# Reading the moving columns of every MLP product alternately from the two halves of their 512

## The chip, the cores and the metric

One NeuronCore of a Trainium2 chip runs the kernel. Its engines are TensorE (PE in the profile; PEld is its loading of weights), VectorE (DVE), ScalarE (ACT), GpSimd (POOL) and SyncE (SP, which issues all the DMAs here). The metric is the device time of one execution in microseconds (us). A matmul multiplies a stationary operand of 128 x 128 with a moving operand of 128 partitions x N columns and writes N columns into one bank of PSUM; the other engines read PSUM and work in SBUF.

## What is computed

Pooled attention, then two MLPs, all in float32. Cut to its core:

```python
k_p = k.reshape(B, H, S // 8, 8, D).mean(axis=3)      # B, H, S, D = 8, 8, 576, 64
v_p = v.reshape(B, H, S // 8, 8, D).mean(axis=3)
attn = softmax(q @ k_p.T / sqrt(D)) @ v_p
x = attn.transpose(0, 2, 1, 3).reshape(4608, 512)
h = x @ w_in;  x = (h * sigmoid(h)) @ w_out           # w_in 512 x 2048, w_out 2048 x 512
h = x @ w_in2; out = (h * clip(h + 3, 0, 6) / 6) @ w_out2
```

## The kernel before

The 4608 tokens are cut into 9 groups of 512 (GT), the 2048 inner columns into 16 slices of 128 (NF). A step is one slice f of one group g of one layer; there are 2 x 9 x 16 = 288 of them, in the order layer, group, slice. The order of all instructions on each engine is written out by hand in the loop at lines 627 to 703.

A float32 value is kept as two float32r parts, a high and a low one (xh and xl, gh and gl, and the two halves of whl for weights), and each product of two such values takes three matmuls: high by high, low by high, high by low.

- h_mm (L410, matmul at L416): the first product of a step. Four blocks of 128 of the 512 inputs by three matmuls, 12 in all, each with a moving operand of 128 x 512: 512 tokens of xh or xl. They add up in one bank, hps; there are two such banks.
- act_a (L425): ScalarE reads the bank into t (L428 in layer 1, L433 in layer 2) and VectorE combines t with the bank (L429, L434). act_b (L439) splits t: ScalarE writes gh (L442), VectorE gl (L443).
- y_mm (L446, matmul at L460): the second product, of the step before; the loop calls it through pend. Four banks y0 to y3 by three matmuls, 12 in all. In layer 1 the weights are stationary and gh or gl (512 tokens) moves, so that the result stands transposed for layer 2; in layer 2 gh or gl is stationary and 512 weight columns move. The four banks add up over the 16 slices of a group.
- y_out (L464) at the end of a group: ScalarE empties y0 and y2 (L469), VectorE y1 and y3 (L471), and SyncE stores them.

So TensorE runs 12 matmuls of h_mm(f), then 12 of y_mm(f-1), then 12 of h_mm(f+1), and the activations of f have all of y_mm(f-1) and h_mm(f+1) to finish in.

Beside the steps of group g in layer 1 the attention of group g+1 is worked, one tile of 128 tokens at a time: scores (L266, matmul L276), the softmax on VectorE and ScalarE (L289 to L329), the transposition (in group 0 by TensorE, L340; later by VectorE, L357, and a way through DRAM), weighted (matmul L380), and split_x (L388), which makes xh (L396) and xl (L397) of the next group. In group 0 the weights of layer 1 come in and are turned from their raw words into high and low parts (L92 to L116); later in layer 1 the same is done for layer 2's weights in pieces (L138 to L158).

At the start, while the first loads arrive, warm_wide (L248) runs matmuls on a tile of zeros, probe, to bring up TensorE's clock: 20 of float32r with 512 columns read straight (L252), 10 of bfloat16 read straight (L254), 10 of float32r whose 512 columns are read alternately from the two halves of the tile (L257), and 10 of bfloat16 with every second word (L259). keep_warm (L261, matmul L264) goes on from there, then come the scores of the first four tiles. pool_k (L193) has filled kbd for them by then, at L206.

Of the kernel before, what the change touches and what calls it, by code (L numbers as in the profile page):

```python
# [12 lines left out]
AF = mybir.ActivationFunctionType  # L13
ALU = mybir.AluOpType
# [10 lines left out]
def kernel(  # L25
# [14 lines left out]
    nc = tc.nc  # L40
    B, NPAIR, P, S = k.shape
# [3 lines left out]
    NF = w_in1.shape[0]  # L45
# [15 lines left out]
    ps_y = ctx.enter_context(tc.tile_pool(name="ps_y", bufs=1, space=PSUM))  # L61
# [4 lines left out]
    three = const.tile([P, 1], F32, name="three")  # L66
# [3 lines left out]
    x1 = [dram.tile([DM, GT], F32, name=f"x1_{g}") for g in range(NG)]  # L70
    blocks = [dram.tile([P, NB, H, Q], F32, name=f"bl{i}") for i in range(2)]
    w2 = [[dram.tile([P, 2, DM], F32, name=f"w2_{f}_{p}") for p in range(2)] for f in range(NF)]


    w_raw = {}
# [164 lines left out]
    def bank(tags, i):  # L240
        pool, tag = tags[i]
        return pool.tile([P, 512], F32, tag=tag, name="aps")
# [2 lines left out]

    probe = p2.tile([P, 512], F32R, tag="o", name="probe", bufs=4)

    def warm_wide(ps, ns):  # L248

        half = probe.bitcast(mybir.dt.bfloat16)  # L250
        for n in range(ns):
            nc.tensor.matmul(ps, probe[:, :P], probe, start=True, stop=True)  # L252
        for n in range(10):
            nc.tensor.matmul(ps, half[:, :P], half[:, :512], start=True, stop=True)  # L254
        two = probe.rearrange("p (a f) -> p f a", a=2)
        for n in range(10):
            nc.tensor.matmul(ps, probe[:, :P], two, start=True, stop=True)  # L257
        for n in range(10):
            nc.tensor.matmul(ps, half[:, :256].rearrange("p (f w) -> p f w", w=2)[:, :, 1], half.rearrange("p (f w) -> p f w", w=2)[:, :, 1], start=True, stop=True)  # L259

    def keep_warm(ps, n):  # L261

# [147 lines left out]
    def h_mm(layer, g, f):  # L410
        ih, il = w_sl[layer, f, 0]
        xh, xl = xs[layer * NG + g]
        ps = ps_h.tile([P, GT], F32, tag="h", name="hps")
        for n, (w, x) in enumerate(((ih, xh), (il, xh), (ih, xl))):
            for c in range(NKC):
                nc.tensor.matmul(  # L416
                    ps,
                    w[:, c, :],
                    x[:, c, :],
                    start=(c == 0 and n == 0),  # L420
                    stop=(c == NKC - 1 and n == 2),
                )
        return ps

    def act_a(layer, ps):  # L425
        t = p2.tile([P, GT], F32, tag="t", name="t")
        if layer == 0:
            nc.scalar.activation(t, ps, AF.Tanh, scale=0.5)  # L428
            nc.vector.scalar_tensor_tensor(  # L429
                out=t, in0=t, scalar=1.0, in1=ps, op0=ALU.add, op1=ALU.mult  # L430
            )
        else:
            nc.scalar.activation(t, ps, AF.Relu, bias=three)  # L433
            nc.vector.scalar_tensor_tensor(  # L434
                out=t, in0=t, scalar=6.0, in1=ps, op0=ALU.min, op1=ALU.mult
            )
        return t

# [7 lines left out]
    def y_mm(layer, g, f):  # L446
        gh, gl = g_t.pop((layer, g, f))
        oh, ol = w_sl[layer, f, 1]
        if f == 0:
            y_ps[layer, g] = [  # L450
                ps_y.tile([P, 512], F32, tag=f"y{i}", name=f"y{i}") for i in range(4)
            ]
        for i, ps in enumerate(y_ps[layer, g]):
            sl = slice(i * P, (i + 1) * P)
            if layer == 0:
                prods = ((oh[:, sl], gh), (ol[:, sl], gh), (oh[:, sl], gl))
            else:
                prods = ((gh[:, sl], oh), (gh[:, sl], ol), (gl[:, sl], oh))
            for n, (a, b) in enumerate(prods):
                nc.tensor.matmul(  # L460
                    ps, a, b, start=(f == 0 and n == 0), stop=(f == NF - 1 and n == 2)
                )

    def y_out(layer, g):  # L464
        scale = 0.5 if layer == 0 else 1.0 / 6.0
        for i, ps in enumerate(y_ps.pop((layer, g))):
            o = p2.tile([P, 512], F32, tag="o", name="o", bufs=4)
            if i % 2 == 0:
                nc.scalar.activation(o, ps, AF.Copy, scale=scale)  # L469
            else:  # L470
                nc.vector.tensor_scalar(  # L471
                    out=o, in0=ps, scalar1=scale, scalar2=None, op0=ALU.mult
                )
            if layer == 0:
                dst = x1[g][i * P:(i + 1) * P, :]
            else:
                dst = out[g * GT + i * P:g * GT + (i + 1) * P, :]
            nc.sync.dma_start(out=dst, in_=o)
# [44 lines left out]
    with tc.manual_schedule():  # L523
# [22 lines left out]
        for i in range(2):  # L546
            nc.gpsimd.memset(kbd[i], 0.0)
        nc.gpsimd.memset(probe.bitcast(F32), 0.0)
        warm_wide(bank(((ps_y, "y0"),), 0), 20)
        make_identity(nc, ident)  # L550
        nc.gpsimd.memset(three, 3.0)
        for i in range(2):
# [74 lines left out]
        for layer in range(2):  # L627
            for g in range(NG):
                todo = stages(g) if layer == 0 else [[] for _ in range(NF)]
                for f in range(NF):  # L630
                    n = (layer * NG + g) * NF + f
# [6 lines left out]
                    while later:  # L638
                        later.pop(0)()
                    ps = h_mm(layer, g, f)  # L640
                    if 1 in now:
                        t1 = now[1]
# [3 lines left out]
                    if 3 in now:  # L646
                        pv = weighted(now[3])
                    tt = act_a(layer, ps)
                    quota = share[n] if n < NF else 2
                    due = len(done)  # L650
# [27 lines left out]
                    if pend is not None:  # L678
                        y_mm(*pend)
                        if pend[2] == NF - 1:  # L680
                            y_out(*pend[:2])
# [8 lines left out]
                    if n >= 5 and layer == 0 and f % 2 == 1:  # L690
# [4 lines left out]
                        if kv_jobs and TPG * (g + 1) + f // 4 + 3 >= first_tile[kv_jobs[0][0]]:  # L695
                            b, j = kv_jobs.pop(0)
# [4 lines left out]
                    if 0 <= s < NF:  # L701
                        load_split(s, 0)
                        load_split(s, 1)
        y_mm(*pend)
        y_out(*pend[:2])


# [46 lines left out]
```

## Time and profile before

| | |
|---|---|
| median of 3 runs | 1772.79 us (1772.59 to 1773.47) |
| the profiled execution | 1772.91 us, its span 1771.1 us |
| granted TensorE clock, mean over the span | 0.994 of full |
| PE busy | 1729.6 us (98%), 8032 matmuls in the records |
| PEld busy | 1388.5 us (78%) |
| DVE busy | 813.2 us (46%) |
| ACT busy | 549.1 us (31%) |
| POOL busy | 254.8 us (14%) |
| MLP matmuls, L416 and L460 | 6912, of 128 x 512 each |

The span is the time from the first to the last instruction of the core; the execution's own time holds some 1.8 us more. Matmuls overlap, so that the mean duration of one is longer than the time from one to the next; the latter is a stretch of the span divided by the matmuls in it. A matmul of plain float32, as those of the attention and of keep_warm, stands in the records as two.

### The profile page before, as it was taken

How to read it: one execution, taken by the hardware profiler on the slowest of the kernel's cores; microseconds unless marked ns; L12 is line 12 of the kernel's file. 1: busy time of each engine (PE TensorE's matmuls, PEld its weight loads, DVE VectorE, ACT ScalarE, POOL GpSimd, SP SyncE). 2: the span in 40 equal slices, each digit the busy share in tenths (PEclk: the TensorE clock that was granted, in tenths of full speed). 3: DMA queues.
4: the chain of work that ended last, by engine and by line, in shares of the span. 5: the costliest groups of instructions: out<-in, count | busy, mean ns of one | idle time of the engine just before them, and what ended most of it. 6: DMA issues, size and time to landing. Idle time of an engine off the chain costs nothing.

```text
span 1771.1 us, 20673 instructions
## 1 busy us (share of the span) xinstructions
PE 1729.6 (98%) x8032; PEld 1388.5 (78%) x8032; DVE 813.2 (46%) x1356; ACT 549.1 (31%) x1007; POOL 254.8 (14%) x258
## 2 busy tenths in 40 slices
PE   8787999999999999999999999999999999999999
PEld 6566887878788888888888888888888888888887
DVE  5999667566665766544322222222222222222222
ACT  4454333333333333222222222222222222222222
POOL 4665222022220222100000000000000000000000
PEclk9899999999999999999999999999999999999999
DMA  8340435343353534211265010101010100000000
GB/s 278 114 163 20 138 123 165 107 144 129 117 168 104 157 124 146 76 67 38 81 200 198 13 36 13 36 13 36 13 36 13 34 14 30 19 22 27 8 17 24
DMA packets 77186, 144.35 MB, mean 82 GB/s; under 512 B 7840, under 2 KB 32288, under 8 KB 77088
## 3 DMA queue, kind: packets, MB, share of 16 engines
q1 hardware_dynamic: 77088, 143.03, 24.7%
q8 instruction: 63, 1.03, 0.3%
q14 instruction: 35, 0.29, 0.1%
HBM read 96.34 MB, written 46.66 MB: 81 GB/s over the span
## 4 chain that ended last, share of the span: by engine, by line
PE 90%; DVE 6%; issue 2%; ACT 1%; POOL 0%; DVEq 0%; ACTq 0%; POOLq 0%
PE y L460 43%; PE hps L416 43%; PE aps L276 2%; PE aps L380 2%; DVE wmag L95 1%; DVE gl L443 1%; DVE wmag L98 1%; DVE t L429 1%; DVE kbd L206 0%; ACT whl L115 0%; PE aps L252 0%; ACT wmag L92 0%; DVE mx L292 0%; DVE den L324 0%; DVE pr L293 0%
## 5 line engine op out<-in xcount | busy, mean ns | idle before, releaser
L416 PE MATMUL hps<-xh,whl 128*128 128x512 f32 x2304 | 585.3, 396 | 3.5 <-POOL whl L116 1.6
L416 PEld LDWEIGHTS hps<-xh,whl 128*128 128x128 f32 x2304 | 434.1, 189 | 107.3 <-POOL whl L116 2.0
L460 PE MATMUL y<-gh,whl 128*128 128x512 f32 x1152 | 372.2, 404 | 1.4 <-POOL whl L116 1.1
L460 PE MATMUL y<-whl,gh 128*128 128x512 f32 x1152 | 361.6, 395 | 0.0
L434 DVE SCALAR_TENSOR_TENSOR t<-t,hps 128x512 f32<-128x512 f32 x144 | 99.1, 688 | 495.4 <-ACT t L433 495.4
L416 PE MATMUL hps<-xl,whl 128*128 128x512 f32 x1152 | 316.1, 396 | 0.8 <-DVE xl L397 0.8
L443 DVE TENSOR_TENSOR gl<-t,gh 128x512 fp32r<-128x512 f32 x288 | 226.7, 787 | 191.2 <-ACT gh L442 190.5
L442 ACT ACTIVATE gh<-t 128x512 fp32r<-128x512 f32 x288 | 182.0, 632 | 269.6 <-DVE t L429 161.0
L416 PEld LDWEIGHTS hps<-xl,whl 128*128 128x128 f32 x1152 | 217.1, 189 | 53.6 <-DVE xl L397 2.1
L460 PEld LDWEIGHTS y<-whl,gh 128*128 128x128 f32 x1152 | 216.3, 188 | 52.3
L460 PEld LDWEIGHTS y<-gh,whl 128*128 128x128 f32 x1152 | 214.2, 190 | 54.4 <-ACT hraw L157 3.7
L433 ACT ACTIVATE t<-hps,three 128x512 f32<-128x512 f32 x144 | 99.1, 688 | 481.4 <-PE hps L416 481.4
L460 PE MATMUL y<-gl,whl 128*128 128x512 f32 x576 | 230.5, 400 | 13.2 <-DVE gl L443 13.2
L460 PE MATMUL y<-whl,gl 128*128 128x512 f32 x576 | 227.4, 395 | 0.0
L429 DVE SCALAR_TENSOR_TENSOR t<-t,hps 128x512 f32<-128x512 f32 x144 | 97.9, 680 | 220.2 <-ACT t L428 219.6
L428 ACT ACTIVATE t<-hps 128x512 f32<-128x512 f32 x144 | 85.9, 596 | 352.9 <-PE hps L416 352.9
L492 POOL TENSOR_TENSOR xl<-xr,xh 128x512 fp32r<-128x512 f32 x36 | 46.5, 1291 | 897.3 <-ACT xh L491 897.3
L460 PEld LDWEIGHTS y<-gl,whl 128*128 128x128 f32 x576 | 109.9, 191 | 41.3 <-DVE gl L443 15.7
L460 PEld LDWEIGHTS y<-whl,gl 128*128 128x128 f32 x576 | 108.2, 188 | 26.0
L158 POOL TENSOR_TENSOR hraw<-hmag,hraw 128x256 fp32r<-128x256 f32 x64 | 47.3, 738 | 424.1 <-ACT hraw L157 328.3
L116 POOL TENSOR_TENSOR whl<-wmag,whl 128x512 fp32r<-128x512 f32 x32 | 50.7, 1601 | 51.9 <-ACT whl L115 51.8
L300 ACT ACTIVATE pr<-pr 128x288 f32<-128x288 f32 x64 | 28.5, 445 | 84.4 <-DVE pr L293 84.4
(78 smaller groups left out, 911.8 us busy)
## 6 DMA issues: line engine op xcount, KB each, us to landing
w<-hraw SPq DMA_DIRECT2D x64, 256.0 KB
whl<-w SPq DMA_DIRECT2D x32, 512.0 KB
bl<-bT SPq DMA_DIRECT2D x28, 384.0 KB
x<-o SPq DMA_DIRECT2D x36, 256.0 KB
xr<-x SPq DMA_DIRECT2D x36, 256.0 KB
out_dram<-o SPq DMA_DIRECT2D x36, 256.0 KB
wraw<-in_moe_w_in_dram SPq DMA_DIRECT2D x16, 512.0 KB
wraw<-in_moe_w_out_dram SPq DMA_DIRECT2D x16, 512.0 KB
```

What stands on the lines that cost most here:

```text
L116: nc.gpsimd.tensor_tensor(out=t[:, 1, :], in0=mag, in1=t[:, 0, :].bitcast(F32), op=ALU.subtract)
L158: nc.gpsimd.tensor_tensor(out=t[:, 1], in0=mag, in1=t[:, 0].bitcast(F32), op=ALU.subtract)
L276: nc.tensor.matmul(ps[o:o + n, jj * PW:(jj + 1) * PW], qT[:, j, o:o + n], kbd[b % 2][:, j, :], start=True, stop=True,)
L416: nc.tensor.matmul(ps, w[:, c, :], x[:, c, :], start=(c == 0 and n == 0), stop=(c == NKC - 1 and n == 2),)
L428: nc.scalar.activation(t, ps, AF.Tanh, scale=0.5)
L429: nc.vector.scalar_tensor_tensor(out=t, in0=t, scalar=1.0, in1=ps, op0=ALU.add, op1=ALU.mult)
L433: nc.scalar.activation(t, ps, AF.Relu, bias=three)
L434: nc.vector.scalar_tensor_tensor(out=t, in0=t, scalar=6.0, in1=ps, op0=ALU.min, op1=ALU.mult)
L442: nc.scalar.activation(gh, t, AF.Copy)
L443: nc.vector.tensor_tensor(out=gl, in0=t, in1=gh.bitcast(F32), op=ALU.subtract)
L460: nc.tensor.matmul(ps, a, b, start=(f == 0 and n == 0), stop=(f == NF - 1 and n == 2))
L492: nc.gpsimd.tensor_tensor(out=xl[:, c, :], in0=r, in1=xh[:, c, :].bitcast(F32), op=ALU.subtract)
```

## The change

Three helpers give other orders to the 512 columns of a tile. shuffled reads column 0, 256, 1, 257 and so on: alternately from the two halves. A matmul whose moving operand is read so writes its 512 results into PSUM in that order, side by side. dealt reads a bank back in the order of the tokens: first every second word from the first on, then every second from the second on. in_two is the plain order, written as two halves so that its shape fits that of dealt.

All MLP matmuls, L416 and L460, now read their moving operand through shuffled. The stationary operands are as before. Every read of a bank of hps or y by ScalarE or VectorE goes through dealt, and what they write in SBUF stands in the old order, so that all else is unchanged. The attention's matmuls are not touched.

The warm-up is another one: 14 float32r matmuls with 512 columns read from the two halves, 10 with 256 columns read from the two halves of 256, and 10 with 512 columns read in turn from the four quarters; no bfloat16 ones. It has 34 matmuls where it had 50. No other instruction of any engine changes its place.

```diff
@@ -70,6 +70,17 @@
     x1 = [dram.tile([DM, GT], F32, name=f"x1_{g}") for g in range(NG)]
     blocks = [dram.tile([P, NB, H, Q], F32, name=f"bl{i}") for i in range(2)]
     w2 = [[dram.tile([P, 2, DM], F32, name=f"w2_{f}_{p}") for p in range(2)] for f in range(NF)]
+    def shuffled(ap):
+        return ap.rearrange("p (a n) -> p n a", a=2)
+    def dealt(ps):
+        return ps.rearrange("p (n a) -> p a n", a=2)
+    def in_two(ap):
+        return ap.rearrange("p (a n) -> p a n", a=2)
 
 
     w_raw = {}
@@ -245,18 +256,17 @@
 
     probe = p2.tile([P, 512], F32R, tag="o", name="probe", bufs=4)
 
-    def warm_wide(ps, ns):
-
-        half = probe.bitcast(mybir.dt.bfloat16)
-        for n in range(ns):
-            nc.tensor.matmul(ps, probe[:, :P], probe, start=True, stop=True)
+    def warm_wide(ps):
+        w = probe[:, :P]
+        for n in range(14):
+            nc.tensor.matmul(ps, w, shuffled(probe), start=True, stop=True)
         for n in range(10):
-            nc.tensor.matmul(ps, half[:, :P], half[:, :512], start=True, stop=True)
-        two = probe.rearrange("p (a f) -> p f a", a=2)
+            nc.tensor.matmul(ps[:, :256], w, shuffled(probe[:, :256]), start=True, stop=True)
         for n in range(10):
-            nc.tensor.matmul(ps, probe[:, :P], two, start=True, stop=True)
-        for n in range(10):
-            nc.tensor.matmul(ps, half[:, :256].rearrange("p (f w) -> p f w", w=2)[:, :, 1], half.rearrange("p (f w) -> p f w", w=2)[:, :, 1], start=True, stop=True)
+            nc.tensor.matmul(
+                ps, w, probe.rearrange("p (a f) -> p f a", a=4), start=True, stop=True
+            )
 
     def keep_warm(ps, n):
 
@@ -416,7 +426,7 @@
                 nc.tensor.matmul(
                     ps,
                     w[:, c, :],
-                    x[:, c, :],
+                    shuffled(x[:, c, :]),
                     start=(c == 0 and n == 0),
                     stop=(c == NKC - 1 and n == 2),
                 )
@@ -424,15 +434,16 @@
 
     def act_a(layer, ps):
         t = p2.tile([P, GT], F32, tag="t", name="t")
+        t2, h = in_two(t), dealt(ps)
         if layer == 0:
-            nc.scalar.activation(t, ps, AF.Tanh, scale=0.5)
+            nc.scalar.activation(t2, h, AF.Tanh, scale=0.5)
             nc.vector.scalar_tensor_tensor(
-                out=t, in0=t, scalar=1.0, in1=ps, op0=ALU.add, op1=ALU.mult
+                out=t2, in0=t2, scalar=1.0, in1=h, op0=ALU.add, op1=ALU.mult
             )
         else:
-            nc.scalar.activation(t, ps, AF.Relu, bias=three)
+            nc.scalar.activation(t2, h, AF.Relu, bias=three)
             nc.vector.scalar_tensor_tensor(
-                out=t, in0=t, scalar=6.0, in1=ps, op0=ALU.min, op1=ALU.mult
+                out=t2, in0=t2, scalar=6.0, in1=h, op0=ALU.min, op1=ALU.mult
             )
         return t
 
@@ -458,7 +469,7 @@
                 prods = ((gh[:, sl], oh), (gh[:, sl], ol), (gl[:, sl], oh))
             for n, (a, b) in enumerate(prods):
                 nc.tensor.matmul(
-                    ps, a, b, start=(f == 0 and n == 0), stop=(f == NF - 1 and n == 2)
+                    ps, a, shuffled(b), start=(f == 0 and n == 0), stop=(f == NF - 1 and n == 2)
                 )
 
     def y_out(layer, g):
@@ -466,10 +477,10 @@
         for i, ps in enumerate(y_ps.pop((layer, g))):
             o = p2.tile([P, 512], F32, tag="o", name="o", bufs=4)
             if i % 2 == 0:
-                nc.scalar.activation(o, ps, AF.Copy, scale=scale)
+                nc.scalar.activation(in_two(o), dealt(ps), AF.Copy, scale=scale)
             else:
                 nc.vector.tensor_scalar(
-                    out=o, in0=ps, scalar1=scale, scalar2=None, op0=ALU.mult
+                    out=in_two(o), in0=dealt(ps), scalar1=scale, scalar2=None, op0=ALU.mult
                 )
             if layer == 0:
                 dst = x1[g][i * P:(i + 1) * P, :]
@@ -546,7 +557,7 @@
         for i in range(2):
             nc.gpsimd.memset(kbd[i], 0.0)
         nc.gpsimd.memset(probe.bitcast(F32), 0.0)
-        warm_wide(bank(((ps_y, "y0"),), 0), 20)
+        warm_wide(bank(((ps_y, "y0"),), 0))
         make_identity(nc, ident)
         nc.gpsimd.memset(three, 3.0)
         for i in range(2):
```

## Rows read from the trace of the kernel before

**Rows 1.** The page: the chain of work that ended last, by line.
```profile
PE y L460 43%; PE hps L416 43%; PE aps L276 2%; PE aps L380 2%; DVE wmag L95 1%; DVE gl L443 1%; DVE wmag L98 1%; DVE t L429 1%; DVE kbd L206 0%; ACT whl L115 0%; PE aps L252 0%; ACT wmag L92 0%; DVE mx L292 0%; DVE den L324 0%; DVE pr L293 0%
```

**Rows 2.** Stretches: bounds, length, busy time (xcount) of each engine, clock, DMA.
```profile
37.00:167.85 130.85, 99.87 (x461) 75.40 (x462) 125.62 (x150) 64.22 (x117) 77.46 (x57) 0.92 0.33 119
167.85:900.00 732.15, 731.37 (x3626) 589.21 (x3626) 441.68 (x834) 237.89 (x475) 117.19 (x138) 1.00 0.37 117
900.00:1771.00 871.00, 867.50 (x3724) 698.90 (x3722) 226.12 (x330) 231.78 (x365) 45.17 (x35) 1.00 0.11 38
11.30:13.46 2.16, 2.16 (x12) 1.66 (x11) 0.00 (x0) 0.00 (x0) 2.00 (x4) 1.00 1.02 263
80.00:160.00 80.00, 63.86 (x336) 49.30 (x334) 76.88 (x96) 40.83 (x75) 44.76 (x33) 1.00 0.29 107
163.50:167.00 3.50, 2.88 (x9) 1.77 (x8) 2.85 (x7) 1.68 (x4) 0.00 (x0) 0.51 0.00 0
```

**Rows 3.** The chain, two blocks: start, us, what.
```profile
412.05 2.80 PE y L460 x12
...
1761.92 5.60 PE y L460 x24
```

**Rows 4.** The chain, the warm-up; second line, the last ten of L252 alone.
```profile
2.34 6.79 PE aps L252 x20
6.82 2.31 PE aps L252 x10
9.13 2.17 PE aps L254 x10
11.30 2.16 PE aps L257 x10
13.46 2.27 PE aps L259 x10
15.73 2.68 PE aps L264 x24
```

**Rows 5.** The same stretch for L416 and for L460 alone: PE, PEld, clock, DMA.
```profile
167.85:1771.00 1603.15, 810.49 (x3288) 617.84 (x3287) 1.00 0.23 74
167.85:1771.00 1603.15, 818.51 (x3300) 616.13 (x3300) 1.00 0.23 74
```

**Rows 6.** Single lines: xcount, ns min/median/max, first and last start.
```profile
L429 DVE SCALAR_TENSOR_TENSOR t<-t,hps x144: 646/689/690, 46.2 to 957.3; 128x512 f32<-128x512 f32 x144
L92 ACT ACTIVATE wmag<-wraw x32: 647/665/698, 32.5 to 168.2; 128x512 f32<-128x512 f32 x32
L115 ACT ACTIVATE whl<-wmag x32: 612/617/632, 35.2 to 174.9; 128x512 fp32r<-128x512 f32 x32
L98 DVE SCALAR_TENSOR_TENSOR wmag<-wraw,wmag x32: 691/694/1715, 33.7 to 171.0; 128x512 uint32<-128x512 uint32 x32
L146 DVE SCALAR_TENSOR_TENSOR hmag<-hraw,hmag x64: 424/425/566, 196.1 to 712.3; 128x256 uint32<-128x256 uint32 x64
```

**Rows 7.** The timeline in layer 2: start, us, engine, what [idle before it].
```profile
1506.84 0.69 DVE L443 TENSOR_TENSOR gl<-t,gh 128x512 fp32r<-128x512 f32 x1 [0.70 <-ACT gh L442]
...
1510.53 0.40 PE L460 MATMUL y<-whl,gl 128*128 128x512 f32 x1
```

**Rows 8.** The timeline of the start.
```profile
9.08 1.51 DVE L206 TENSOR_REDUCE kbd<-stage 64x72 f32<-64x576 f32 x2 [1.42 <-DMA stage<-in_k_dram]
10.57 1.26 POOL L216 TENSOR_TENSOR stage<-stage 72x512 f32<-72x512 f32 x1 [4.06 <-DMA stage<-in_v_dram]
```

**Rows 9.** The timeline in layer 1.
```profile
162.39 0.50 PE L460 MATMUL y<-gl,whl 128*128 128x512 f32 x1 [3.85 <-DVE gl L443]
...
280.63 1.19 PE L416 MATMUL hps<-xl,whl 128*128 128x512 f32 x4 [0.23 <-DVE xl L397]
...
415.66 0.69 DVE L443 TENSOR_TENSOR gl<-t,gh 128x512 fp32r<-128x512 f32 x1 [0.70 <-ACT gh L442]
...
417.96 0.40 PE L460 MATMUL y<-gl,whl 128*128 128x512 f32 x1
```

## The prediction, made before the changed kernel ran

> **What bounds the kernel now.** I read the chain that ended last first. 86% of the span run through the two MLP lines on TensorE, L416 and L460, and 4% more through its attention lines [rows 1]. The reader is to see there that no other engine, and no transfer, holds the end.
>
> A table by stretch then says where that is not so [rows 2]. From 37 to 168 us VectorE is busy 125.6 of 130.9 us and TensorE 99.9. VectorE is converting weights and doing attention beside the first steps, and TensorE waits for it. From 167.85 us on TensorE is busy all the time (731.4 of 732.2 us, then 867.5 of 871, the rest being the last evacuation and store) at a granted clock of 1.00. There the time is the number of matmuls times their pace.
>
> The pace is the number to look at. A row's "mean ns of one" (395 to 404 ns) is no pace, since matmuls overlap. From 900 us to 1767.52, where the last block ends, there are 3724 matmuls [rows 2, 3], which makes 233.0 ns from one to the next; a block of 12 in layer 1 takes 2.80 us, which is 233 ns too [rows 3].
>
> **The change, part by part.**
>
> *The moving reads.* The warm-up before the first real work happens to hold the operation that is now put everywhere [rows 4]. Its first loop has the same matmul as the MLP (float32r, 128 x 512, read straight): once the clock is up ten of them take 2.31 us, 231 ns each, on zeros. The third loop reads the same tile alternately from its two halves: ten take 2.16 us, 216 ns each. Ten straight bfloat16 ones take 2.17 us. So a straight float32r read costs some 15 to 17 ns per matmul that the alternating one does not. That the zeros of the probe pace like the real work when read straight (231 against 233) is my reason to carry the 216 over.
>
> The price: after 167.85 us there are 3288 matmuls of L416 and 3300 of L460 [rows 5], 6588. At 233 - 216 = 17.0 ns each that is 112.0 us. The other 324 (of 288 steps of 24) lie before it and gain nothing, because VectorE sets the time there. Bounds on the new pace: below, the row's own 216, since bfloat16 comes to the same 216 or 217; above, 227, the slowest full-clock group of the warm-up (strided bfloat16, 2.27 us for ten), if the reads meet traffic that the probe lacked; at 227 the gain is 40 us. I take 216, the one row of this very form.
>
> [...] The probe's row shows the scattered read faster than the straight one, 2.16 against 2.31 us for ten [rows 4]. [...]
>
> *The dealt reads of PSUM.* Per step ScalarE and VectorE read the first product's bank once each (VectorE's L429 takes 0.689 us [rows 6]), and per group of 16 steps they empty two of the four y banks each. All now read every second word. The trace has no strided read of PSUM. The nearest rows are strided reads of SBUF: L92 on ScalarE, every second word, 0.665 against 0.617 us for L115, which reads straight; L98 on VectorE, 0.694, against 0.689 for L429 [rows 6]. So the low bound is nothing (a gain is excluded: the same number of elements is read), the next +0.05 us, and the far one a doubling of the part that grows with the elements. That part I get from one shape against half its size: L98's 0.694 us for 512 and L146's 0.425 for 256 [rows 6], 0.27 us per 256, so +0.54 us for 512. I take nothing to 0.05, by the nearest rows. What covers it: in layer 2 gl, the last of the four passes that follow the product, is done at 1506.84 + 0.69 = 1507.53 us, while the matmul that needs it starts at 1510.53 [rows 7]: 3.0 us to spare, 2.6 after 24 matmuls at 17 ns less. Without that cover each step would pay. In the stretch to 167.85 us VectorE has no cover, and 13.5 steps (324 matmuls by 24 a step) would pay 13.5 x 0.54 = 7.3 us at the far bound.
>
> *The warm-up.* Before, it runs from 2.34 to 15.73 us [rows 4], and the chain goes straight through it. Now: 14 matmuls of 512 columns (the first ten 4.48 us, as before, 6.82 - 2.34, then four at 216), ten of 256 and ten of 512 read from four quarters. A 256-column one lies between the 128-column row (2.68 us for 24, 112 ns) and 216; I take 130. The quarters I take at 216, with twice that as the far bound. Sum 4.48 + 0.86 + 1.3 + 2.16 = 8.8 us against 13.39, so 4.6 us less (1.6 us with both far bounds). What is late next? The scores need kbd, whose last reduction ends at 9.08 + 1.51 = 10.6 us [rows 8], and q; the warming at L264 (2.68 us) still lies between, so they start at about 13.8 us. The loads of q and v are queued alternately and v's first lands at 10.57 us [rows 8]; five more of some 0.26 to 0.29 MB at the 263 GB/s of that stretch [rows 2] bring the last q to about 15.7 us, when the fourth tile's scores come at 16.8. So it fits, barely, and the 4.6 us move the VectorE stretch forward whole.
>
> *What closes in.* With TensorE 7% quicker its waits for others grow. At three ends of a group in layer 1 it already waits for VectorE's xl, 0.23 us in the first of them, at 280.63 [rows 9]; the path before it holds 20 matmuls (12 of y, 8 of xh), so 0.33 us more each: 1.0 us. The tightest place otherwise is VectorE's softmax step: gl is done at 415.66 + 0.69 = 416.35 us and wanted at 417.96 [rows 9], 1.6 us; of the two steps from the scores to there 48 matmuls get quicker by 0.8 us. Half of the slack is left, so nothing is charged. VectorE is busy 442 of 732 us from 167.85 to 900; with 2864 matmuls of the two lines there (6588 less 3724) the stretch gets 49 us shorter, and VectorE is busy 65% of it.
>
> The sum, against the profiled execution's 1772.9 us (the median is 0.1 lower): 1772.9 - 112.0 - 4.6 + 1.0 = 1657.3, say 1657.
>
> **The rivals.**
>
> *The evacuations double.* For it: no row shows a strided PSUM read. [...] Against it: SBUF's strided reads cost at most 0.05 us. Price: 7.3 us up to 167.85 us; in layer 1, two dearer reads in the softmax step's path (1.08 us against 0.8 of slack), 0.28 us in each of the 28 tiles of groups 1 to 7's attention, 7.8. 1657 + 15 = 1672. It does not eat the gain.
>
> *Only part of it comes.* With VectorE and ScalarE at work the pace is that of the strided bfloat16 row, 227: 6588 x 6 ns = 40 us; 1772.9 - 4.6 - 40 = 1728.
>
> [...]
>
> *Slower.* In 11.3 to 13.46 us VectorE and ScalarE are at 0.00 [rows 2]; in the kernel they are busy 60 and 32% of the time from 167.85 to 900 us and 26 and 27% from 900 on. If the alternating reads collide with their reads and writes of SBUF where straight ones do not, the pace rises above 233. It decides from 233.7 ns on (4.6 us over 6588). The nearest price is what striding did to bfloat16 beside POOL and DMA alone, 227 against 217: 10 ns on top of 233 gives 1772.9 - 4.6 + 66 = 1834. [...] Against it: POOL (2.00 of 2.16 us) and the DMA engines (1.02) were busy during the probe, and the straight pace is the same in layer 1 and layer 2 although VectorE is more than twice as busy in the first.
>
> **The clock.** In the VectorE stretch TensorE's idle pieces grow by up to 24 x 17 ns = 0.4 us. [...] I charge nothing, and leave 6 us in the range.
>
> **How the numbers follow.** Forecast 0.75, its own range 1650 to 1668; evacuations doubled 0.11; part of it 0.05; pace unchanged 0.05; slower 0.04. The range 1646 to 1684 holds the forecast and the doubled evacuations with the clock's 6 us on top, and leaves out the other three and the tails. A difference under 0.2% (3.5 us) cannot be told from none; the unchanged pace at 1768 lies just past that line, so I split it. Faster 0.75 + 0.11 + 0.05 + 0.02 = 0.93, the same 0.03, slower 0.04.
>
> **What would show it.** Blocks of 12 matmuls in the chain at 2.59 us instead of 2.80, and the last 3724 matmuls in 804 us instead of 867.5. L429, L434, L428 and L433 within 0.05 us of before. The first scores at 13.8 us instead of 18.24. TensorE waits for xl of 0.6 us at group ends. I am wrong if the blocks stay at 2.80 us or go over, or if VectorE holds TensorE beyond 168 us.

## The result, and the profile after

The changed kernel takes 1669.08 us (median of 4 runs, 1667.22 to 1669.66) where the kernel before takes 1773.13 (4 runs, 1772.59 to 1773.91): a ratio of 0.9411, 95% interval 0.9395 to 0.9427. The forecast was 1657, so it lies inside the range of 1646 to 1684, 12 us later than the forecast itself and 1 us above the forecast's own range of 1650 to 1668. By the number alone it lies nearer to the doubled evacuations (1672) than to the forecast; the lines have to tell the two apart. These 12 us are what the experiments look for.

The profiled execution took 1669.22 us, its span 1667.4. First the chain that ended last, by line and then its blocks (start, us, what). Lines have moved: L416 is now L426, L460 is L471; L92, L98, L105 and L115 are L103, L109, L116 and L126.

```profile
PE y L471 41%; PE hps L426 40%; PE aps L390 1%; PE aps L286 1%; DVE wmag L109 1%; DVE wmag L106 1%; DVE gl L454 1%; DVE wmag L116 1%; DVE t L440 1%; DMA wraw<-in_moe_w_out_dram 1%; DMA hraw<-in_moe_w_out_dram 1%; DMA stage<-in_v_dram 1%; DMA stage<-in_q_dram 1%; DMA bl<-bT 0%; DMA wraw<-in_moe_w_in_dram 0%
```

```profile
902.08 2.59 PE y L471 x12
904.67 2.59 PE hps L426 x12
...
1658.36 5.39 PE y L471 x24
```

A block of 12 takes 2.59 us instead of 2.80 [rows 3]: 216 ns from one matmul to the next, as the alternating row of the warm-up had it [rows 4]. The MLP lines still hold the end, but their share fell from 86% [rows 1] to 81%, and of VectorE's conversions L116 (before: L105) now stands at 1% beside L106 and L109, which had that before (L95, L98).

The same by stretch (bounds, length, then busy time of PE, PEld, DVE, ACT, POOL; clock, DMA share, GB/s):

```profile
37.00:168.20 131.20, 96.13 (x450) 76.66 (x449) 126.36 (x145) 64.81 (x113) 77.87 (x56) 0.87 0.31 114
168.20:900.00 731.80, 726.87 (x3815) 625.78 (x3813) 455.48 (x850) 257.45 (x494) 119.46 (x140) 1.00 0.40 129
900.00:1667.40 767.40, 763.73 (x3538) 668.20 (x3536) 215.13 (x314) 220.65 (x347) 42.05 (x33) 1.00 0.10 31
```

Against [rows 2] the reader sees two things. From 168 us on TensorE is idle for 4.9 of 731.8 us where it was idle for 0.8. And up to 168 us no more was done than before, though the change was to bring this stretch forward by 4.6 us: the row has 450 matmul records against 461, but 11 have only moved ahead of 37 us, and in either kernel the 325th MLP matmul starts at about 168 us (below). What TensorE waits for from 168 to 900 us (total, times, longest):

```profile
PE hps L426 <- DVE xl L407: 1.8, 3, 0.7
PE aps L390 <- DMA pT<-bl: 1.8, 2, 1.2
PE y L471 <- POOL whl L127: 0.5, 1, 0.5
PE aps L390 <- ACT pT L351: 0.3, 1, 0.3
PE aps L286 <- DVE xl L407: 0.2, 1, 0.2
```

Single lines (min/median/max in ns): the two that read PSUM dealt out, then the conversions, which read every second word of SBUF, and one that reads straight:

```profile
L440 DVE SCALAR_TENSOR_TENSOR t<-t,hps x144: 647/687/690, 44.1 to 913.2; 128x512 f32<-128x512 f32 x144
L482 DVE TENSOR_SCALAR o<-y x36: 680/682/692, 188.2 to 1663.8; 128x512 f32<-128x512 f32 x36
L103 ACT ACTIVATE wmag<-wraw x32: 647/724/928, 30.0 to 168.9; 128x512 f32<-128x512 f32 x32
L109 DVE SCALAR_TENSOR_TENSOR wmag<-wraw,wmag x32: 693/844/1818, 31.1 to 170.9; 128x512 uint32<-128x512 uint32 x32
L157 DVE SCALAR_TENSOR_TENSOR hmag<-hraw,hmag x64: 424/503/595, 196.6 to 686.1; 128x256 uint32<-128x256 uint32 x64
L126 ACT ACTIVATE whl<-wmag x32: 612/614/634, 32.6 to 175.8; 128x512 fp32r<-128x512 f32 x32
```

The reads of PSUM cost what they cost before (L429: 0.689 us at the median, [rows 6]). But three of these lines, which the change does not touch, got slower: L92 from 665 to 724 ns, L98 from 694 to 844, L146 from 425 to 503; L115, which reads side by side, stayed (617, 614). That is where the theory came from.

One line that reads side by side got slower too, VectorE's shift between the two strided passes (before, after):

```profile
L95 DVE TENSOR_SCALAR wmag<-wmag x32: 413/428/1944, 33.2 to 170.6; 128x512 uint32<-128x512 uint32 x32
L106 DVE TENSOR_SCALAR wmag<-wmag x32: 412/606/1915, 30.7 to 170.4; 128x512 uint32<-128x512 uint32 x32
```

Two early ones make the difference: at 36.62 and 39.11 us L106 met a GpSimd instruction that had begun 0.2 us earlier and took 1.39 and 1.35 us, where its counterparts took 0.43 and 1.04. The strided lines L109 and L116 (50 operations) sum to 57.5 us instead of 53.9, L106 (32) to 25.9 instead of 24.7. In e10 below, where the strided reads are quick again, these are back at 53.7 and 24.5, so L106's share follows from the strided ones.

**Where the 12 us are.** From the starts of the 6912 MLP matmuls I take the first, the 325th (from which on TensorE no longer waits for VectorE's work of the first stretch) and the last:

| | before | after | forecast | missed |
|---|---|---|---|---|
| first MLP matmul | 36.85 | 34.29, so -2.56 | -4.6 | 2.0 |
| first to 325th | 130.75 | 133.89, so +3.1 | 0 | 3.1 |
| 325th to last | 1599.51 | 1495.17, so -104.3 | -111.0 | 6.7 |

What follows the last matmul takes 4.0 and 4.1 us. The middle row alone is longer than before; the steady part holds the greater miss.

### The profile page after: what moved, and what is told of

Its sections match the earlier page's. It is cut to its first block, busy times and chain, and to the rows that moved or that the text cites. A ratio compares the mean times of both kernels' runs of the same rounds, so it can differ in the third digit from the quotient of the medians.

```text
span 1667.4 us, 20343 instructions
## 1 busy us (share of the span) xinstructions
PE 1615.8 (97%) x8016; PEld 1395.7 (84%) x8016; DVE 820.8 (49%) x1356; ACT 560.6 (34%) x1007; POOL 255.1 (15%) x258
## 4 chain that ended last, share of the span: by engine, by line
PE 84%; DVE 8%; DMA 4%; issue 2%; ACT 1%; SPq 1%; POOL 0%; DVEq 0%; POOLq 0%; ACTq 0%
PE y L471 41%; PE hps L426 40%; PE aps L390 1%; PE aps L286 1%; DVE wmag L109 1%; DVE wmag L106 1%; DVE gl L454 1%; DVE wmag L116 1%; DVE t L440 1%; DMA wraw<-in_moe_w_out_dram 1%; DMA hraw<-in_moe_w_out_dram 1%; DMA stage<-in_v_dram 1%; DMA stage<-in_q_dram 1%; DMA bl<-bT 0%; DMA wraw<-in_moe_w_in_dram 0%
## 5 line engine op out<-in xcount | busy, mean ns | idle before, releaser
L426 PE MATMUL hps<-xh,whl 128*128 128x512 f32 x2304 | 546.4, 380 | 4.2 <-POOL whl L127 2.1
L426 PEld LDWEIGHTS hps<-xh,whl 128*128 128x128 f32 x2304 | 435.9, 189 | 67.4 <-POOL whl L127 2.5
L471 PE MATMUL y<-gh,whl 128*128 128x512 f32 x1152 | 357.4, 392 | 1.6 <-POOL whl L127 1.2
L471 PE MATMUL y<-whl,gh 128*128 128x512 f32 x1152 | 342.6, 379 | 0.0
L454 DVE TENSOR_TENSOR gl<-t,gh 128x512 fp32r<-128x512 f32 x288 | 221.1, 768 | 190.5 <-ACT gh L453 190.5
L426 PE MATMUL hps<-xl,whl 128*128 128x512 f32 x1152 | 296.8, 380 | 1.8 <-DVE xl L407 1.8
L471 PEld LDWEIGHTS y<-gh,whl 128*128 128x128 f32 x1152 | 217.2, 193 | 39.3 <-issue 3.7
L426 PEld LDWEIGHTS hps<-xl,whl 128*128 128x128 f32 x1152 | 218.1, 190 | 34.0 <-DVE xl L407 3.0
L471 PEld LDWEIGHTS y<-whl,gh 128*128 128x128 f32 x1152 | 217.7, 189 | 30.9
L444 ACT ACTIVATE t<-hps,three 128x512 f32<-128x512 f32 x144 | 99.2, 689 | 422.2 <-PE hps L426 422.2
L471 PE MATMUL y<-gl,whl 128*128 128x512 f32 x576 | 223.4, 388 | 13.5 <-DVE gl L454 13.4
L471 PE MATMUL y<-whl,gl 128*128 128x512 f32 x576 | 218.4, 379 | 0.0
L439 ACT ACTIVATE t<-hps 128x512 f32<-128x512 f32 x144 | 85.8, 596 | 260.8 <-PE hps L426 260.6
L471 PEld LDWEIGHTS y<-gl,whl 128*128 128x128 f32 x576 | 111.2, 193 | 33.3 <-DVE gl L454 17.1
L471 PEld LDWEIGHTS y<-whl,gl 128*128 128x128 f32 x576 | 108.9, 189 | 15.8 <-DVE gl L454 0.3
```

The source lines that it names most:

```text
L426: nc.tensor.matmul(ps, w[:, c, :], shuffled(x[:, c, :]), start=(c == 0 and n == 0), stop=(c == NKC - 1 and n == 2),)
L439: nc.scalar.activation(t2, h, AF.Tanh, scale=0.5)
L444: nc.scalar.activation(t2, h, AF.Relu, bias=three)
L454: nc.vector.tensor_tensor(out=gl, in0=t, in1=gh.bitcast(F32), op=ALU.subtract)
L471: nc.tensor.matmul(ps, a, shuffled(b), start=(f == 0 and n == 0), stop=(f == NF - 1 and n == 2))
```

## The experiments

Theory: alternating reads from columns that lie far apart leave TensorE fast but slow the strided SBUF reads of VectorE and ScalarE beside them, and this lengthens the stretch that VectorE sets. Rivals: the clock after the new warm-up, the dealt PSUM reads, or the pace itself.

**e0_pace**, a kernel of its own that leaves out the whole computation: blocks of 24 matmuls of 128 x 512 float32r on random data, one order of columns each, then VectorE and ScalarE beside two of them.

```python
def halves(t): return t.rearrange("p (a n) -> p n a", a=2)
def apart(n):  return lambda t: t.rearrange("p (m a n) -> p m n a", a=2, n=n)
def second(t): return t.rearrange("p (n a) -> p a n", a=2)
def pairs(t):  return t.rearrange("p (a n b) -> p n a b", a=2, b=2)
```

> A kernel of its own: it leaves out the whole computation and runs 24 float32r matmuls of 128 x 512 on random data in each of several column orders, and 110 in each of two orders with VectorE and ScalarE reading SBUF beside them, side by side or every second word. Theory (the alternating read is quick by its two places 256 columns apart, and in exchange it slows other engines' reads of every second word): straight 231 to 233 ns, halves 216, quarters about 274 as in the warm-up; beside halves VectorE's read of every second word takes 0.84 instead of 0.69 us and ScalarE's 0.72 instead of 0.65, reads side by side stay; beside the straight order nothing changes. Rival (the dearer reads come from something else of the whole kernel, GpSimd or the loads): the same durations in both blocks. If any two places far enough apart will do, the orders that alternate 16 to 128 columns apart take 216 too; if only 256 columns do, they take 233 or more.

Its chain: straight, halves, quarters, every second column, four and four from the halves, two and two, then alternating 4 columns apart; last the two long blocks with the engines beside, straight and halves.

```profile
42.09 5.44 PE ps L127 x24
47.53 5.18 PE ps L129 x24
52.71 6.79 PE ps L131 x24
59.50 10.83 PE ps L133 x24
70.33 6.00 PE ps L135 x24
76.33 8.15 PE ps L137 x24
84.49 5.18 PE ps L139 x24
...
126.46 24.94 PE ps L157 x110
151.62 23.76 PE ps L161 x110
```

Halves take 5.18 / 24 = 216 ns, straight 227, quarters 283, every second column 451, two and two 340. Alternating 4, 8, 16, 32, 64 or 128 columns apart gives 5.18 us, all the same, so in the orders tried not the halves matter but that each column comes from another place than its neighbour, two places in turn. Work beside did not change the pace (23.76 / 110 = 216). What changed was the work: a strided VectorE read took 691 to 694 ns beside straight matmuls and 828 to 852 beside halves, ScalarE's 656 to 667 and 884 to 903 (720 was expected), while side-by-side reads kept their 680 to 694 and 613 to 632. So the collision that the prediction's last rival names exists, with the roles turned round. The straight pace here is 227, in the kernel 233; that difference stays open.

**e1_warm_up_alone** is the kernel before with the new warm-up, **e2_old_warm_up** the changed kernel with the old one.

```diff
 e1: -  ps, a, shuffled(b), ...        +  ps, a, b, ...        (and all reads straight)
 e2: -  new warm_wide                  +  the 20, 10, 10, 10 matmuls of before
```

> Only the new warm-up, MLP products as before. Theory: the first scores at 13.8 us, the first MLP product 2.5 us earlier than before, VectorE's stretch no longer than before since no matmul reads alternately in it: 2.5 us won, 1770.6 us against 1773.1. Rival (the earlier start alone puts VectorE and GpSimd out of step and lengthens the stretch by the 3 us seen): 1773 to 1774.

> The whole change but for the warm-up, which is the old one. Theory (the stretch up to 168 us is longer because strided conversions are slowed by the alternating matmuls): the stretch still takes 3 us longer, so the time is that of the changed kernel plus 2.5, 1671.6 us. Rival (the earlier start is to blame for the longer stretch): 1668 to 1669, no worse than the changed kernel.

e1: 1770.4 us, ratio 0.9983 (0.9973 to 0.9993); its first MLP matmul starts at 34.73 us, 2.1 earlier than before. e2: 1670.38, ratio 0.942 (0.9406 to 0.9434). From first to 325th matmul e1 needs 130.7 us, e2 134.0. So the lengthening goes with the MLP reads and not with the warm-up, as the theory wants. The total of e2 decides nothing: it lies between the two expectations, because its steady part came out 2.2 us shorter than that of the changed kernel.

**e5_layer_2_alone**: alternation in layer 2 only, where nothing is converted.

```diff
-    shuffled(x[:, c, :]),
+    shuffled(x[:, c, :]) if layer else x[:, c, :],
```

> Columns read alternately (and dealt out) in layer 2 alone, with the new warm-up. Theory: VectorE's and ScalarE's reads of every second word (L109, L153, L157; L103, L149) go back to 0.69, 0.43, 0.43, 0.66 and 0.42 us, TensorE's waits in layer 1 to those of before; 3456 matmuls x 17 ns = 58.8 us and the start's 2.5 are won: 1712 us. Rival (the dearer reads come from the new start or from other engines): they stay at 0.84, 0.49, 0.50, 0.72 and 0.51 in layer 1 and the time is 1714 or more.

1711.34 us, ratio 0.965 (0.9636 to 0.9664). Blocks of 12 take 2.59 us in layer 2 and 2.79 in layer 1, and L103 and L157 are back at 660 and 425 ns. The first stretch takes 130.7 us.

**e3_side_by_side**: the changed kernel, its conversions reading contiguous words and ScalarE's first pass a constant, so that the weights are other numbers; the amount of work is the same. **e4_before_side_by_side** does the same to the kernel before.

```diff
-        raw = wts.tile([P, DM, 2], U32, ...)       +        raw = wts.tile([P, 2, DM], U32, ...)
-        hw = raw[:, :, 1]                          +        hw = raw[:, 1, :]
```

> The whole change, but the conversions of the weights read words that lie side by side: VectorE takes the first or second 512 words of a raw tile instead of every second one, ScalarE reads a constant; so the weights are other numbers and only the time counts. Theory (reads of every second word, slowed by the alternating matmuls, lengthen VectorE's stretch by 3 us and some of layer 1's waits): L-lines of the conversions at 0.69 and 0.43 us, the first 324 MLP matmuls done at 165 us instead of 168.2, time 1664 to 1666 us. Rival (the waits come from TensorE's pace alone): 1668 to 1669.

> The control: the kernel before with the same conversions that read words side by side (the weights are other numbers). Theory: beside straight matmuls the reads of every second word cost nothing, so 1773 us as before, within 1 us. Rival (side by side is quicker in itself): 1770 or less.

e3: 1664.87 us, ratio 0.9388 (0.9374 to 0.9402), 4.2 us under the changed kernel (the intervals just overlap); 3.4 of them are in the first stretch, which takes 130.5 us. VectorE's conversion (L115 there) takes 694 ns at the median beside the same alternating matmuls. e4: 1773.17, ratio 0.9997 (0.9988 to 1.0007): side by side is worth nothing when the matmuls read straight. So the 3.1 us of the stretch hang on strided reads beside alternating ones. Whether the rest of the 4.2 does is not shown: the steady part alone differs by up to 3.1 us between profiles of one order (e10 to e12 below).

**e6_psum_straight**: the changed kernel with PSUM read straight, so that the columns of the result stand in another order.

```diff
-        return ps.rearrange("p (n a) -> p a n", a=2)
+        return in_two(ps)
```

> The whole change, but hps and y are read from PSUM word after word, so that the columns of each group stand in another order in the result. Theory (dealing costs nothing): 1669 us as the changed kernel, within 1 us, and the four activation lines at the same durations. Rival (dealt reads cost VectorE and ScalarE something): 1666 or less.

1669.66 us, ratio 0.9414 (0.94 to 0.9428), and the lines of above again:

```profile
L440 DVE SCALAR_TENSOR_TENSOR t<-t,hps x144: 647/686/691, 44.1 to 913.9; 128x512 f32<-128x512 f32 x144
L482 DVE TENSOR_SCALAR o<-y x36: 678/681/693, 188.1 to 1664.5; 128x512 f32<-128x512 f32 x36
```

Dealing the columns out at the read costs nothing, within 2 ns a line (ScalarE's L439, L444 and L480 as well: 597, 689 and 588 ns against 597, 689 and 587).

**e0b_beside**, again without the computation: 130 matmuls each of straight, halves, 4, 16 and 128 columns apart, and the same reads of the other engines beside each, to see whether the distance between the two places matters.

> A kernel of its own again (it leaves out the whole computation): beside 130 matmuls in each of five column orders run VectorE, then ScalarE, then GpSimd, with reads of every word, every second and every fourth. The alternation 4, 16 and 128 columns apart had the same 216 ns as halves. [...] Theory B (the distance matters): the near ones, 4 or 16 apart, slow them less. [...]

VectorE's four reads of every second word beside the five orders, in the order named, one row each (bounds, length, VectorE's busy time, clock, DMA share, GB/s):

```profile
47.00:76.00 29.00, 2.77 (x4) 1.00 0.00 1
76.50:104.00 27.50, 3.31 (x4) 1.00 0.00 1
104.80:132.40 27.60, 2.77 (x4) 1.00 0.00 1
133.00:160.60 27.60, 2.77 (x4) 1.00 0.00 1
161.40:189.00 27.60, 3.35 (x4) 1.00 0.00 0
```

All four alternating orders run at 216 ns. Beside halves (256 columns apart) and 128 apart a strided read takes 0.83 us; beside 4 and 16 apart it takes 0.69, as beside straight. ScalarE goes the same way: 0.85 to 0.89 us beside halves and 128 apart, 0.65 to 0.67 beside 4 and 16, 0.64 to 0.66 beside straight. GpSimd's strided read stays at 1.29 to 1.30 us beside all five. So the distance decides, and a version without this cost suggests itself. Where between 16 and 128 the border lies, and why distance matters, no run shows.

**e10_apart_4** is that version.

```diff
-        return ap.rearrange("p (a n) -> p n a", a=2)
+        return ap.rearrange("p (m a n) -> p m n a", a=2, n=4)
...
-        t2, h = in_two(t), dealt(ps)
+        t2, h = t, ps
...
-        nc.scalar.activation(gh, t, AF.Copy)
+        nc.scalar.activation(in_two(gh), dealt(t), AF.Copy)
```

The dealing moves from the reads of hps to those of t, for gh and gl; as e6 has shown, the reads of PSUM were not dear.

> The whole change kept, but all MLP moving columns are read alternately from places 4 columns apart (four-by-four exchange inside each 8) instead of 256 apart; h stays in PSUM's order through act_a and is dealt in act_b. In the runs of pace, columns 4 apart gave 215.8 ns as the halves did and left strided reads of VectorE at 691-693 ns (halves: 827-829). Theory (the 12 us missed come in part from strided reads slowed beside alternation between distant columns): conversions back at 647-698 ns, matmul 324 at or before 165.4 us (after: 168.2), end 3 to 5 us before the changed kernel: 1664-1666 us. Rival (the first stretch is set by the clock or by the pace, or the dealt reads of act_b cost as much): matmul 324 at 168 and 1668-1670 us or more.

1662.17 us (1660.44 to 1664.22), ratio 0.9373 (0.9361 to 0.9386): faster than both kernels, its interval clear of the changed kernel's. The first of its lines here is the chain, then its two conversions:

```profile
849.23 2.59 PE hps L426 x12
```

```profile
L103 ACT ACTIVATE wmag<-wraw x32: 647/664/683, 28.2 to 163.5; 128x512 f32<-128x512 f32 x32
L109 DVE SCALAR_TENSOR_TENSOR wmag<-wraw,wmag x32: 691/693/1701, 29.4 to 166.2; 128x512 uint32<-128x512 uint32 x32
```

The pace is kept and the conversions are back where they were. gh, now read out of order, takes 681 instead of 629 ns (288 times, hidden on ScalarE); gl stays at 693. The gain is more than the 3 to 5 us expected. In the profile, the quickest of the four executions, 3.5 us come from the stretch, 1.7 from the start and 3.5 from the steady part, of which only the first is explained by the distance: e11 and e12 below have the same steady part and take 1494.8 and 1493.1 us for it, where e10 takes 1491.7 and the changed kernel 1495.2.

**e8_group_0_straight**: the changed kernel, but the MLP products of group 0 of layer 1 read straight.

```diff
-                    shuffled(x[:, c, :]),
+                    shuffled(x[:, c, :]) if alt(layer, g) else x[:, c, :],
...
+        return layer > 0 or g > 0
```

The last line is the body of alt; y_mm and the reads of PSUM follow it in the same way.

> The changed kernel, but the MLP products of the first group of layer 1 (the stretch to matmul 576) read their moving columns in order, 256-apart alternation begins with the second group. Theory (strided conversions are slowed while matmuls alternate between distant columns): conversions before 168 us back to 647-698 ns, first stretch 130.7 us instead of 133.9, matmul 324 at 165.2; from there to the group's end about 250 matmuls at 227 instead of 215.8, partly given back: 2.8 us lost; net 1668-1669.5, so little in the total, all in where matmul 324 stands. Rival (the stretch is longer by the clock after the warm-up, or by the pace): matmul 324 stays at 168 and the total is 1671-1672.

1666.76 us (1664.74 to 1670.17), ratio 0.9404 (0.9391 to 0.9417). The 325th matmul starts at 164.19 us, and the stretch is at 130.7 us. A slower pace of TensorE gave a shorter stretch, so the pace does not set it. The total came out 1 to 3 us under the expectation; its interval overlaps that of the changed kernel, so what counts is the stretch.

The stretch from the first to the 325th matmul in one view (columns as above): before, after, e8, e10.

```profile
36.85:167.61 130.76, 99.78 (x461) 75.31 (x461) 125.53 (x150) 64.13 (x116) 77.61 (x57) 0.92 0.33 120
```

```profile
34.29:168.19 133.90, 98.82 (x461) 78.84 (x461) 128.72 (x149) 67.45 (x116) 78.76 (x57) 0.87 0.32 118
```

```profile
33.50:164.19 130.69, 101.61 (x460) 76.68 (x461) 125.48 (x149) 64.04 (x116) 77.73 (x57) 0.90 0.33 122
```

```profile
32.57:162.92 130.35, 99.94 (x461) 79.67 (x461) 125.12 (x150) 64.94 (x116) 76.52 (x57) 0.87 0.33 122
```

VectorE is idle for 5.2 us in each; its busy time rose by 3.2 us (125.53 to 128.72) and the stretch by 3.1. e10 has the changed kernel's clock, 0.87, and the short stretch, which clears the clock. The other runs fall in line: 133.9 to 134.3 us where the conversions are slow (after, e2, e6), 130.1 to 130.9 in all that have them fast.

**e11_apart_4_short_warm_up** and **e12_apart_4_max_on_scalar** change the start of e10.

```diff
 e11: -  for n in range(10): nc.tensor.matmul(ps, w, probe.rearrange("p (a f) -> p f a", a=4), ...)
 e12: -  nc.vector.tensor_scalar(out=mx, in0=mx, scalar1=-ESCALE, scalar2=None, op0=ALU.mult)
      +  nc.scalar.activation(mx, mx, AF.Copy, scale=-ESCALE)
```

> As the kernel with columns 4 apart, without the ten quarter-order matmuls of the warm-up (24 matmuls left of 34). In the changed kernel the warm-up ends at 11.15 and scores start at 13.83. Theory (quarters at 274 instead of 216 cost 0.6 us, but scores wait for VectorE's chain from then on): 0 to 1.5 us earlier than the kernel with columns 4 apart, the first MLP matmul moves by less than the 2.7 us taken out. Rival (the quarters keep the clock up): scores run at the lower clock and the first MLP matmul is later by 1 us or more.

> As the kernel with columns 4 apart, with the scaling of the row maxima (a small tensor_scalar of VectorE, 0.76 and 1.19 us in the changed kernel, 0.17 in the kernel before) moved to ScalarE. Theory (VectorE's small operation is held up beside GpSimd's tensor_tensors, since the scores now run 4.4 us earlier, and this is where 2 of the 4.6 us of the warm-up went): first MLP matmul 1 to 1.6 us earlier than 34.3, total 1 to 1.6 us less than the kernel with columns 4 apart. Rival (the stretch to 168 us is VectorE's and begins with its own work): first matmul earlier, but matmul 324 where it was, total the same within 0.5 us.

e11: 1662.97 us, ratio 0.9377 (0.9364 to 0.9389). The first MLP matmul starts at 31.86 us, 0.7 before that of e10, less than the 2.7 taken out, as the theory wants; the total, 0.8 us over that of e10, shows nothing of it. Its scores did not slow down for want of the quarters, against the rival: the granted clock is 1.00 from 11.94 to 31.86 us. e12: 1661.35 us (1661.23 to 1661.6), ratio 0.9369 (0.9356 to 0.9381): the lowest median, 0.8 us under e10, too little to tell from it. Its first MLP matmul starts at 32.38 us, 1.9 before the changed kernel's but only 0.2 before that of e10. What e12 does show is the wait itself. In the changed kernel, VectorE's small L317 beside GpSimd's pooling of v (start, us, engine):

```profile
15.33 1.26 POOL L227 TENSOR_TENSOR stage<-stage 72x512 f32<-72x512 f32 x1
...
15.87 0.76 DVE L317 TENSOR_SCALAR mx<-mx 128x4 f32<-128x4 f32 x1
```

```profile
17.97 1.26 POOL L227 TENSOR_TENSOR stage<-stage 72x512 f32<-72x512 f32 x1
...
18.07 1.19 DVE L317 TENSOR_SCALAR mx<-mx 128x4 f32<-128x4 f32 x1
```

The same operation in the kernel before, at its later place, and on ScalarE in e12:

```profile
21.90 0.17 DVE L307 TENSOR_SCALAR mx<-mx 128x4 f32<-128x4 f32 x1
```

```profile
16.06 1.26 POOL L227 TENSOR_TENSOR stage<-stage 72x512 f32<-72x512 f32 x1
...
16.23 0.21 ACT L317 ACTIVATE mx<-mx 128x4 f32<-128x4 f32 x1
```

In the changed kernel both end 0.02 to 0.03 us after the GpSimd instruction beside which they started (16.60, 19.23). In the eight profiles with the new warm-up and VectorE's form this holds for all 15 that met one, and what they lose differs from run to run, 0.2 to 1.9 us over the two. From the first scores to the first MLP matmul it is 18.6 us before, 19.1 to 20.8 in those eight, and 18.2 in e12. That goes with the loss: 20.5 us where L317 loses 1.6 (the changed kernel), 20.8 where it loses 1.9 (e1), 19.1 where it loses 0.2 (e10). In the changed kernel L335 and L339 of the first tile, 0.34 and 0.84 us instead of 0.17 and 0.76, lose the 0.25 that is left of its 1.85.

## Why the prediction was right, and where it missed

- **The pace** was right: 216 ns, in both layers, on real data and beside busy engines. Between MLP matmuls that follow each other directly (6530 pairs from the 325th on) it is 232.8 ns before and 215.8 after, longer stops left out. The rivals with half the gain, none or a loss fell with it, and layer 2 alone brought its share (e5: 1711 us, 1712 expected). The 1768 of an unchanged pace no run shows: with the pace of before, the new warm-up alone came to 1770.4 (e1).
- **The dealt PSUM reads** were right at nothing (e6), and with that the rival of doubled evacuations fell, though the total came close to its 1672.
- **The sum of the warm-up** was right: its end came at 11.15 us as added up, though ten quarters took 2.74 us instead of 2.16 and the rest less; the scores started at 13.83 (forecast 13.8). The failed step is the one behind it, "the 4.6 us move the VectorE stretch forward whole". I asked whether q would be there, and not what ran beside VectorE in the new place: 4.41 us earlier at the scores, less 1.85 us between scores and first MLP matmul, are 2.56. Twice L317 started beside a GpSimd instruction and ended 0.02 to 0.03 us after it; why it is held up, no run shows. 0.76 and 1.19 us instead of 0.17 are its price here.
- **The VectorE stretch** is the step that failed in kind: the 324 matmuls "gain nothing", right, but I weighed only PSUM reads and the clock for the stretch and charged nothing. Its strided SBUF reads, with the waits of L106 that follow from them, became a term of 3.1 us. The 325th matmul was to start at 163.0 us (167.61 less 4.6) and started at 168.19, at the very line that the prediction drew as a sign of being wrong ("if VectorE holds TensorE beyond 168 us"). The prediction's last rival named this collision and let TensorE pay; VectorE and ScalarE pay: in e0_pace VectorE's strided read takes 691 to 694 ns beside straight matmuls and 828 to 852 beside halves, ScalarE's 656 to 667 and 884 to 903.
- **xl** was right: the three waits at group ends make 1.1 us more than before, start to start and at the new pace; forecast 1.0.
- **The clock** was lower in the stretch (0.87 against 0.92) and cost nothing that shows: e10 has 0.87 too, and its stretch takes 130.35 us. The 6 us that the range leaves for the clock no run shows. Nor does a run show that the warm-up brings the clock up: in the kernel before it is granted at 1.00 from 0 to 16 us, while the first ten matmuls take 4.48 us and ten later ones of the same loop 2.31 [rows 4].
- **The steady part** missed 6.7 us. The direct pairs saved 106.8 of the 111.0 us that 6530 x 17.0 makes: 0.3 is pace and 3.9 longer stops (11.7 us over the pace in 85 pairs, before 7.8 in 66), of which xl is 1.1. Of the rest, 0.8 are three stops before the first y matmul after a group's end, beside y_out, with none there before; 0.5 is the wait for GpSimd's whl; some 1.0 lie at and behind matmuls that read gl, for which half of the slack was to be left. The 57 pairs with attention between them grew by 2.5 us where 1.0 less was implied; two waits for the transfer of pT, 1.8 us, make most of it. So 7.7 us went missing, of which 1.0 was forecast. All of it lies in layer 1: the matmuls of layer 2, from the first to the last, take 745.9 us instead of 805.2, 59.3 less, and 17.0 ns each make 58.7. The waits for pT are 2.3 us in the profile of e3, and 0, 2.1 and 0.4 in those of e10, e11 and e12, all with fast conversions, so slow conversions are not their cause. What is stays open, and with it the greatest of the three misses.

## What to carry to other kernels

An edit that only changes the order in which one engine reads SBUF can be paid by another engine (here 3.1 us of VectorE's stretch): list the strided reads that run beside it, and measure them beside the new order. If alternating reads are faster, choose the two places close together rather than half a tile apart (here a strided read of VectorE took 0.69 us beside 4 and 16 columns, 0.83 beside 256). And when a stretch is moved earlier, look at what the other engines do at its new place, small operations too.

## What the hardware showed

- Float32r matmuls of 128 x 512 follow each other at 216 ns when neighbouring columns are read in turn from two places 4 to 256 columns apart, at 227 (here alone) to 233 ns (in the kernel) when read straight.
- Beside such matmuls with places 128 or 256 columns apart, reads of every second word take 0.83 us on VectorE instead of 0.69 and 0.85 to 0.90 on ScalarE instead of 0.64 to 0.67; beside places 4 or 16 apart they stay at 0.69 and 0.65 to 0.67 us. Contiguous reads take 680 to 694 ns on VectorE and 613 to 632 on ScalarE, beside straight matmuls and beside halves (e0_pace). GpSimd's reads of every second word take 1.29 to 1.30 us beside all of these. Reading every fourth word (256 elements) also takes 0.83 us beside halves, against 0.61 beside straight ones.
- Reads of every second word of PSUM take VectorE and ScalarE as long as straight ones, within 2 ns (687 against 686 and 682 against 681 ns on VectorE; 597 and 689 in both on ScalarE).
- A VectorE operation of 128 x 4 (0.17 us) that started while a GpSimd instruction ran ended 0.02 to 0.03 us after that one, 15 times of 15 in the eight profiles with the new warm-up; on ScalarE it takes 0.21 us beside the same.
